# A chunked attention followed by two MLPs on one core: ScalarE's later-block step moved behind unit 1's casts, and six more products of constants on TensorE

## The chip, the cores and the metric

One core of a Trainium2 chip. The metric is the device time of one execution in microseconds (us); the median of several executions is given. TensorE (PE) multiplies matrices, VectorE (DVE), ScalarE (ACT) and GpSimd (POOL) work on tiles, SyncE (SP) issues most of the loads. Each engine takes its instructions strictly in the order in which the program has them and waits for the others by semaphores.

## What is computed

Three stages, one behind the other, all in fp32:

```python
log_a = np.log(np.clip(a, 1e-06, 1.0))            # attention: 4 batches, 8 heads, 768 steps, chunks
for c in range(nc):
    cum = np.cumsum(la, axis=-1)
    L = np.exp(cum[:, :, :, None] - cum[:, :, None, :]) * causal
    M = np.einsum('bhin,bhjn->bhij', Cc, Bc) * L
    y[:, :, sl] = np.einsum('bhij,bhjd->bhid', M, xc) \
        + np.einsum('bhin,bhnd->bhid', Cc, state) * np.exp(cum)[:, :, :, None]
    state = decay_full[:, :, None, None] * state + np.sum(Bx, axis=2)
...
out1 = (silu(x @ w_gate) * (x @ w_val)) @ w_out   # x: 3072 x 256, inner width 1536
...
out[mask] = gate_w[mask, None] * (np.maximum(out1[mask] @ w1[e], 0.0) @ w2[e])   # 8 experts, top 1
```

## The kernel before

The 3072 tokens are cut into 24 **units** of 128 (`NU`) and 6 **blocks** of 512 (`BLK`), four units to a block. A unit goes through: `weigh` (L273, inputs times decay weights: tile xw), `scores_mm` (L286 and L292, 32 small matmuls: the chunk's state sums and C times B), `scores_m` (L300, the causal mask: tile mt), `values_mm` (L338 and L348, 64 small matmuls), `values_out` (L364 to L367, decays put on: tiles y and z; then L369, ScalarE's cast of the unit's output to fp32r: the upper half of xt), `states` (L316, L319 on VectorE, L321, L322 on ScalarE) and `values_low` (L375, the lower half of xt, what the cast left). The MLPs then run each fp32 product as three fp32r products of upper and lower halves.

`first_block` has a **pre-phase** of units 0 to 3, which is all that block 0 needs, and behind it a loop over the MLP's steps of blocks 0 and 1, among which units 4 to 11 are put. In the pre-phase the decays are set up too: `setup_cum(0, 1)` computes for blocks 0 and 1 the exponentials of sums of logarithms (two matmuls passes to a block pair at L192, an exponential on ScalarE at L194: tile er), `setup_cum(1, 2)` those for blocks 2 to 5. `emit_d(b)` spreads er over four rows of constants (tile du; for b = 0 on GpSimd at L254, for b = 1 by four activations on ScalarE at L252), and `emit_u(b, d)` turns that by two matmuls (L265) and two copies on ScalarE (L266) into U, the factor of the unit's outputs. The MLP's weights arrive as 64-bit words, and `decode` makes fp32 of them in four parts: 0 on ScalarE (L400), 1 on VectorE (L403, L404, L406), 2 on ScalarE (L409: wh), 3 on VectorE (L411: wl). `silu_first` (L210) loads ScalarE's table for Silu ahead of its first use. `load(u)` issues two DMAs on SP.

`keep_busy(n)` issues n matmuls of 512 columns on constants (L203), each into the same PSUM tile that nobody reads. They are there for TensorE's clock, which the chip holds at one of two levels, 1.2 and 2.4 GHz; the profile calls the granted level the granted clock (0.50 and 1.00).

The order is written by hand (`manual_schedule`): each engine's queue holds its instructions as the calls below come. Tiles of one `tag` share `bufs` buffers in the order in which they are made, and a new one waits until the readers of the one before it in that buffer are done. Three facts of that kind touch the change: the tag "mt" (two buffers) holds eh, the masked scores of every unit and du; the tag "g" in PSUM (three buffers) holds the results of `setup_cum`, `emit_u` and half of `values_mm`; xt of block 0 is read by the first MLP matmul (L431), which stands behind the last `keep_busy`.

Of the kernel before, what the change touches and what calls it, by code (L numbers as in the profile page):

```python
# [120 lines left out]
def kernel(  # L121
# [17 lines left out]
    def ps_g(name, shape=(128, BLK)):  # L139
        return ps.tile(list(shape), F32, tag="g", bufs=3, name=name)  # L140
# [21 lines left out]
    def load(u):  # L162
        if u >= NU or u in raw:
            return
        r = {}
        xbb = ap_.tile([128, 512], F32, name="xbb", tag="xbb", bufs=4)
        nc.sync.dma_start(out=xbb, in_=I["xbb"][:, u])
        r["x"] = xbb[:, 0:DM].rearrange("k (h d) -> k h d", h=8)
        r["b"] = xbb[:, DM:DM + 128]
        r["bt"] = xbb[:, DM + 128:]  # L170
        r["c"] = ap_.tile([128, 2, 4, 64], F32, name="cbd", tag="cbd", bufs=4)
        nc.sync.dma_start(out=r["c"].rearrange("p r h i -> p (r h i)"), in_=I["cbd"][:, u])
        raw[u] = r

    def setup_loads():
        nc.sync.dma_start(out=at, in_=I["at"])
        nc.scalar.dma_start(out=c1, in_=I["cst"][:, 0:C1])

    def setup_ln():
        nc.vector.tensor_scalar(out=at, in0=at, scalar1=1e-6, scalar2=1.0, op0=ALU.max, op1=ALU.min)  # L180
        nc.scalar.activation(out=at, in_=at, func=AF.Ln)

    def setup_decay():
        p = ps_g("pw", (128, NBLK, 32))
        nc.tensor.matmul(out=p, lhsT=c1[:, C_S:C_S + 128], rhs=at[:, :, 0:32], start=True, stop=True)
        nc.scalar.activation(out=W, in_=p, func=AF.Exp)

    def setup_cum(b0, n):

        p = ps_g("pe", (128, n, 132))  # L190
        for b in range(n):
            nc.tensor.matmul(out=p[:, b], lhsT=at[:, 2 * (b0 + b):2 * (b0 + b) + 2].rearrange("k b c -> k (b c)"),  # L192
                             rhs=c1[:, C_S:C_S + 132], start=True, stop=True)
        nc.scalar.activation(out=er[:, b0:b0 + n], in_=p, func=AF.Exp, scale=-1.0)  # L194
# [3 lines left out]
    def keep_busy(n):  # L198

        if not idle_t:  # L200
            idle_t.append(ps.tile([128, 2, 256], F32, tag="y0", bufs=1, name="pi"))
        for _ in range(n):
            nc.tensor.matmul(out=idle_t[0], lhsT=r32[:, 0],  # L203
                             rhs=r32.rearrange("p g j -> p (g j)").unsqueeze(1).to_broadcast([128, 2, 256]),
                             start=True, stop=True)

    def silu_first():

        t = ap_.tile([128, 1], F32, name="sf")
        nc.scalar.activation(out=t, in_=c1[:, C_ME:C_ME + 1], func=AF.Silu)  # L210

    def setup_ones():
        nc.vector.tensor_copy(out=r16, in_=c1[:, C_R16:C_R16 + 128])
        nc.vector.tensor_copy(out=r32, in_=c1[:, C_R32:C_R32 + 256].rearrange("p (g j) -> p g j", g=2))
# [25 lines left out]
    def cum_store(b0, n, p):  # L240
        nc.vector.tensor_copy(out=eb[:, 8 * b0:8 * b0 + 8 * n], in_=p)
# [5 lines left out]
    def emit_d(b):  # L247
        d = ap_.tile([128, 4, 128], F32R, name="du", tag="mt", bufs=2)
        o = C_MU + 4 * (b % 2)
        if b in (1, 2):  # L250
            for q in range(4):
                nc.scalar.activation(out=d[:, q], in_=er[:, b // 2, 0:128], func=AF.Copy, scale=c1[:, o + q:o + q + 1])  # L252
        else:
            nc.gpsimd.tensor_tensor(  # L254
                out=d, in0=er[:, b // 2, 0:128].unsqueeze(1).to_broadcast([128, 4, 128]),
                in1=c1[:, o:o + 4].unsqueeze(2).to_broadcast([128, 4, 128]), op=ALU.mult)
        return d
# [10 lines left out]
    def weigh(u, e):  # L268

        r = raw[u]  # L270
        b, o = divmod(u, 4)
        r["xw"] = ap_.tile([128, 8, 32], F32, name="xw", tag="xw", bufs=3)
        e.tensor_tensor(out=r["xw"], in0=r["x"], in1=W[:, b, o * 8:o * 8 + 8].unsqueeze(2).to_broadcast([128, 8, 32]),  # L273
                        op=ALU.mult)
# [107 lines left out]
    def load_w(f, e=nc.sync):  # L382
        if f >= NF:
            return
        wr[f] = keep.tile([128, 768, 2], I32, name="wraw", tag="raw", bufs=3)
        e.dma_start(out=wr[f], in_=I["mw"][f].bitcast(I32).rearrange("p (n t) -> p n t", t=2))
# [403 lines left out]
    def first_block():  # L790

        setup_loads()
        load(0)
        load_w(0)
        load(1)
        load(2)
        load_w(1)
        load(3)
        load_w(2)
        nc.sync.dma_start(out=c2, in_=I["cst"][:, C1:C_END])  # L800
        load_w(3)
        setup_ln()
        setup_ones()
        setup_decay()
        setup_cum(0, 1)
        keep_busy(2)
        weigh(0, nc.vector)
        scores_mm(0)
        cum_split(0, 1)
        scores_m(0)  # L810
        emit_u(0, emit_d(0))
        cum_store(0, 1, cum_ends(0, 1, cum_ends_d(0, 1)))
        states(0)
        cum_pairs(1, 8)
        keep_busy(3)
        decode(0, 0)
        for u in range(4):
            weigh(u + 1, nc.vector)
            scores_mm(u + 1)
            values_mm(u)  # L820
            if u == 1:
                setup_cum(1, 2)
            if u == 1:
                d = emit_d(1)
            if u == 2:
                emit_u(1, d)
            keep_busy((5, 7, 6, 10)[u])
            decode(u // 2, 3 if u % 2 else 1)
            scores_m(u + 1)
            if u % 2 == 0:  # L830
                decode(u // 2, 2)
            values_out(u)
            states(u + 1)
            values_low(u)
            if u % 2:
                decode(u // 2 + 1, 0)
            load(u + 4)
            if u == 1:
                silu_first()
        load_w(4)  # L840

        todo = {0: 2, 1: 3, 2: 4, 4: 5, 6: 6, 8: 7, 10: 8, 12: 9, 14: 10, 15: 11}
        units = {0: 4, 1: 5, 3: 6, 5: 7, 13: 8, 16: 9, 19: 10, 22: 11}
        for i in range(2 * NF):
            q, f = divmod(i, HALF)
            b, f = q % 2, f + HALF * (q // 2)
            u = units.get(i)
            w = todo.get(i, NF)
            if i + 1 in units and units[i + 1] > 4:
                weigh(units[i + 1] + 1, nc.vector if i < 16 else nc.gpsimd)  # L850
            if i == 0:
                weigh(5, nc.vector)
            if u == 7:
                scores_mm(u + 1)
                values_mm(u)
                values_out(u)
                values_low(u)
            p = mlp1_mm(b, 0, BLK, f)
            if u is not None and u != 7:
                scores_mm(u + 1)  # L860
                values_mm(u)
            if len(late) == LAG:
                mlp1_down(*late.pop(0))
            late.append((b, 0, BLK, f))
            decode(w, 1)
            h = mlp1_h(p, BLK)
            if w < NF:
                load_w(w + 3)
                decode(w + 1, 0)
            decode(w, 2)  # L870
            if u is not None and u != 7:
                values_out(u)
            decode(w, 3)
            if i >= 20:
                turn_y(0, i - 20)
            mlp1_split(h, b, 0, BLK, f)
            if i in (7, 13):
                take_part(0 if i == 7 else 1)
            if i == 19:
                take_y(0)  # L880
            if u is not None:
                if u != 7:
                    values_low(u)
                    scores_m(u + 1)
                    states(u + 1)
                load(u + 4)
            if i == 6:
                scores_m(8)
                cum_split(1, 2)
            if i == 7:  # L890
                dd.append(cum_ends_d(1, 2))
            if i == 8:
                cum_store(1, 2, cum_ends(1, 2, dd.pop()))
                cum_pairs(8, NU)
                states(8)
            if i == 9:
                dd.append(emit_d(2))
            if i == 10:
                emit_u(2, dd.pop())
            if 16 <= i < 20:  # L900
                setup_route(i - 16)
            if i == 21:
                dd.append(emit_d(3))
            if i == 23:
                emit_u(3, dd.pop())
# [193 lines left out]
```

## Time and profile before

| | us |
|---|---|
| median of 3 executions | 546.77 |
| lowest, highest | 545.44, 546.95 |
| the profiled execution | 547.26 |
| its span, first to last instruction | 545.5 |
| TensorE busy in it | 512.3 (94%) |
| VectorE | 297.8 (55%) |
| ScalarE | 212.7 (39%) |

The profile is of one execution, and its times count from the start of the span. A busy TensorE need not be one at its peak, since matmuls are pipelined. "Issue" in the chain is time in which the engine waited for nothing that the profile shows. The mean granted clock was 0.981.

### The profile page before, as it was taken

How to read it: one execution, taken by the hardware profiler on the slowest of the kernel's cores; microseconds unless marked ns; L12 is line 12 of the kernel's file. 1: busy time of each engine (PE TensorE's matmuls, PEld its weight loads, DVE VectorE, ACT ScalarE, POOL GpSimd, SP SyncE). 2: the span in 40 equal slices, each digit the busy share in tenths (PEclk: the TensorE clock that was granted, in tenths of full speed). 3: DMA queues.
4: the chain of work that ended last, by engine and by line, in shares of the span. 5: the costliest groups of instructions: out<-in, count | busy, mean ns of one | idle time of the engine just before them, and what ended most of it. 6: DMA issues, size and time to landing. Idle time of an engine off the chain costs nothing.

```text
span 545.5 us, 11245 instructions
## 1 busy us (share of the span) xinstructions
PE 512.3 (94%) x4597; PEld 422.2 (77%) x4597; DVE 297.8 (55%) x648; ACT 212.7 (39%) x394; POOL 97.5 (18%) x120
## 2 busy tenths in 40 slices
PE   5699899999999999999999999999997999999990
PEld 3477688778877778887788778888895999899980
DVE  4888787775453554445444554454463755646320
ACT  4644356433232334333433233434442443544320
POOL 0000000121003040004100034211036324250211
PEclk9899899999999999999999999999998999999996
DMA  8755222111030212103100104334056635431100
GB/s 309 263 175 193 100 100 93 40 50 40 22 99 0 62 60 40 40 20 99 21 1 2 41 2 142 92 117 40 20 175 78 186 94 157 146 117 45 38 15 28
DMA packets 20551, 45.85 MB, mean 84 GB/s; under 512 B 4624, under 2 KB 8080, under 8 KB 20496
## 3 DMA queue, kind: packets, MB, share of 16 engines
q1 hardware_dynamic: 17280, 38.39, 23.0%
q0 software_dynamic: 3072, 6.41, 4.5%
q8 instruction: 37, 0.61, 0.6%
q10 hardware_dynamic: 144, 0.30, 0.2%
q14 instruction: 18, 0.15, 0.1%
HBM read 38.59 MB, written 6.50 MB: 83 GB/s over the span
## 4 chain that ended last, share of the span: by engine, by line
PE 76%; issue 11%; DVE 5%; POOL 2%; ACT 2%; DMA 1%; another core or an unknown queue 0%; SPq 0%; POOLq 0%; ACTq 0%
PE py L459 18%; PE pg L431 18%; PE pv L431 17%; PE ph L741 7%; PE po L762 6%; PE pt L543 2%; PE pc L292 2%; POOL out L776 2%; PE py L348 1%; PE py L338 1%; PE pi L203 1%; PE pc L286 1%; PE px L730 1%; DVE hl L446 1%; DMA at<-in_at 1%
## 5 line engine op out<-in xcount | busy, mean ns | idle before, releaser
L431 PE MATMUL pg<-xt,wh 128*128 128x512 f32 x288 | 93.5, 406 | 1.8 <-ACT wh L409 1.8
L431 PE MATMUL pv<-xt,wh 128*128 128x512 f32 x288 | 91.0, 397 | 0.4 <-DVE h L439 0.2
L439 DVE TENSOR_TENSOR h<-h,pv 128x512 f32<-128x512 f32 x72 | 49.4, 686 | 64.1 <-PE pv L431 53.1
L446 DVE TENSOR_TENSOR hl<-h,hh 128x512 fp32r<-128x512 f32 x72 | 50.1, 695 | 62.6 <-ACT hh L445 62.3
L762 PE MATMUL po<-hl,hh 128*128 128x256 f32 x384 | 70.7, 284 | 3.3 <-ACT hh L749 3.3
L741 PE MATMUL ph<-xt,hl 128*128 128x512 f32 x288 | 73.9, 399 | 0.0
L431 PEld LDWEIGHTS pv<-xt,wh 128*128 128x128 f32 x288 | 54.4, 189 | 14.0 <-DVE h L439 0.6
L762 PEld LDWEIGHTS po<-hl,hh 128*128 128x128 f32 x384 | 60.5, 190 | 5.8 <-ACT hh L749 3.8
L431 PEld LDWEIGHTS pg<-xt,wh 128*128 128x128 f32 x288 | 52.4, 190 | 12.4 <-ACT wh L409 2.0
L445 ACT CAST hh<-h 128x512 fp32r<-128x512 f32 x72 | 44.6, 620 | 39.0 <-DVE h L439 39.0
L741 PEld LDWEIGHTS ph<-xt,hl 128*128 128x128 f32 x288 | 52.4, 191 | 9.4
L438 ACT ACTIVATE h<-pg 128x512 f32<-128x512 f32 x72 | 42.7, 593 | 42.0 <-PE pg L431 41.9
L459 PE MATMUL py<-hh,wh 128*128 128x512 f32 x144 | 58.6, 407 | 0.0
L431 PE MATMUL pg<-xt,wl 128*128 128x512 f32 x144 | 57.5, 399 | 0.0
L459 PE MATMUL py<-hl,wh 128*128 128x512 f32 x144 | 56.9, 395 | 0.0
L459 PE MATMUL py<-hh,wl 128*128 128x512 f32 x144 | 56.9, 395 | 0.0
L431 PE MATMUL pv<-xt,wl 128*128 128x512 f32 x144 | 56.8, 394 | 0.0
L601 POOL DMA_INDIRECT slots<-ids,si x24 | 25.4, 1058 | 167.1 <-DVE si L593 162.3
L762 PE MATMUL po<-hl,hl 128*128 128x256 f32 x192 | 54.2, 282 | 0.4 <-DVE hl L750 0.4
L750 DVE SCALAR_TENSOR_TENSOR hl<-ph,hh 128x512 fp32r<-128x512 f32 x48 | 33.1, 689 | 35.5 <-ACT hh L749 33.7
L749 ACT ACTIVATE hh<-ph 128x512 fp32r<-128x512 f32 x48 | 28.8, 600 | 42.3 <-PE ph L741 21.3
L762 PEld LDWEIGHTS po<-hl,hl 128*128 128x128 f32 x192 | 36.2, 189 | 0.9 <-DVE hl L750 0.9
(140 smaller groups left out, 672.0 us busy)
## 6 DMA issues: line engine op xcount, KB each, us to landing
eraw<-in_ew SPq DMA_DIRECT2D x24, 512.0 KB
wraw<-in_mw SPq DMA_DIRECT2D x12, 768.0 KB
xbb<-in_xbb SPq DMA_DIRECT2D x24, 256.0 KB
cbd<-in_cbd SPq DMA_DIRECT2D x24, 256.0 KB
yd<-yr SPq DMA_DIRECT2D x6, 528.0 KB
slots<-ids,si POOLq DMA_INDIRECT x24
xg<-yd,idx POOLq DMA_INDIRECT x24
out<-ob,idx POOLq DMA_INDIRECT x24
```

Of the source, the lines that this page charges most:

```text
L292: nc.tensor.matmul(out=r["pc"][g][32 * q:32 * q + 32, 0:256], lhsT=r["bt"][k, 32 * q:32 * q + 32], rhs=r["c"][k, q // 2].rearrange("p h i ...
L431: nc.tensor.matmul(out=t, lhsT=w[:, f, o:o + 128], rhs=xt[:, xp, k, cs], start=n == 0, stop=n == 5)
L438: nc.scalar.activation(out=h, in_=p[0], func=AF.Silu)
L439: nc.vector.tensor_tensor(out=h, in0=h, in1=p[1], op=ALU.mult)
L445: nc.scalar.copy(out=hh, in_=h)
L446: e.tensor_tensor(out=hl, in0=h, in1=hh.bitcast(F32), op=ALU.subtract)
L459: nc.tensor.matmul(out=yb[b][d][:, c:c + m], lhsT=w[:, f, o:o + 128], rhs=h, start=first and n == 0, stop=last and n == 2, skip_group_chec ...
L601: i = nc.gpsimd.indirect_dma_start(out=slots[0:E * upto], out_offset=bass.IndirectOffsetOnAxis(ap=si[:, s:s + 1], axis=0), in_=ids[g][:, o ...
L741: nc.tensor.matmul(out=p, lhsT=self.hl[:, w, o:o + 128], rhs=self.xt[:, xp, k], start=n == 0, stop=n == 5)
L749: nc.scalar.activation(out=hh, in_=p, func=AF.Relu)
L750: nc.vector.scalar_tensor_tensor(out=hl, in0=p, scalar=0.0, in1=hh.bitcast(F32), op0=ALU.max, op1=ALU.subtract)
L762: nc.tensor.matmul(out=self.po[s // 2][:, s % 2], lhsT=h[:, q], rhs=self.hl[:, w, o:o + DM], start=f == 0 and n == 0 and s % 2 == 0, stop= ...
```

## The change

In the loop over the pre-phase's four units, `setup_cum(1, 2)` and `emit_d(1)` are taken from behind the value matmuls of unit 1 and put, in the other order, at the end of that pass, behind unit 1's output, the states, `values_low`, the first decode step of the next weights and the load of unit 5, and ahead of `silu_first`. On TensorE the two matmuls of `setup_cum(1, 2)` thereby come behind `keep_busy` of unit 1 instead of ahead of it. The counts of `keep_busy` go from 2 to 3, 3 to 4, and in the loop from 5, 7, 6, 10 to 7, 8, 7, 10: six products more in all.

```diff
@@ -803,7 +803,7 @@
         setup_ones()
         setup_decay()
         setup_cum(0, 1)
-        keep_busy(2)
+        keep_busy(3)
         weigh(0, nc.vector)
         scores_mm(0)
         cum_split(0, 1)
@@ -812,19 +812,15 @@
         cum_store(0, 1, cum_ends(0, 1, cum_ends_d(0, 1)))
         states(0)
         cum_pairs(1, 8)
-        keep_busy(3)
+        keep_busy(4)
         decode(0, 0)
         for u in range(4):
             weigh(u + 1, nc.vector)
             scores_mm(u + 1)
             values_mm(u)
-            if u == 1:
-                setup_cum(1, 2)
-            if u == 1:
-                d = emit_d(1)
             if u == 2:
                 emit_u(1, d)
-            keep_busy((5, 7, 6, 10)[u])
+            keep_busy((7, 8, 7, 10)[u])
             decode(u // 2, 3 if u % 2 else 1)
             scores_m(u + 1)
             if u % 2 == 0:
@@ -836,6 +832,8 @@
                 decode(u // 2 + 1, 0)
             load(u + 4)
             if u == 1:
+                d = emit_d(1)
+                setup_cum(1, 2)
                 silu_first()
         load_w(4)
```

## Rows read from the trace of the kernel before

**Rows 1.** The page's head: the span.

```profile
span 545.5 us, 11245 instructions
```

**Rows 2.** The chain that ended last, 4 to 36 us: start, us, what.

```profile
14.05 2.42 issue
...
17.79 0.45 PE py L338 x29
...
18.72 1.04 PE pe L192 x4
...
22.54 0.32 PE pc L286 x10
...
23.29 0.32 PE py L338 x24
...
24.00 0.66 PE pu L265 x2
...
26.04 1.71 issue
...
29.22 2.50 PE pi L203 x10
31.72 1.38 PE pg L431 x6
```

**Rows 3.** Stretches: bounds, us; busy us of each engine (instructions); PEclk, DMA share, GB/s.

```profile
14.10:16.50 2.40, 0.03 (x5) 0.06 (x6) 2.37 (x11) 1.47 (x4) 0.00 (x0) 0.91 1.03 389
16.50:19.50 3.00, 3.00 (x100) 2.49 (x101) 1.91 (x6) 0.00 (x0) 0.00 (x0) 0.50 1.01 393
19.80:26.25 6.45, 5.08 (x111) 3.64 (x109) 4.98 (x14) 6.42 (x14) 0.00 (x0) 1.00 0.48 148
40.00:60.00 20.00, 17.16 (x310) 13.10 (x293) 18.08 (x38) 10.02 (x19) 0.00 (x0) 1.00 0.39 134
60.10:64.80 4.70, 4.66 (x13) 3.24 (x14) 2.76 (x7) 1.47 (x3) 0.00 (x0) 0.64 0.80 279
```

**Rows 4.** TensorE's instructions, 6 to 10 us: start, us, engine, line, operation, tiles.

```profile
6.25 0.78 PE L203 MATMUL pi<-r 128*128 128x512 f32 x1
6.83 0.63 PE L203 MATMUL pi<-r 128*128 128x512 f32 x1
7.39 0.47 PE L286 MATMUL pc<-xw,xbb 64*32 64x64 f32 x16
...
9.80 0.25 PE L236 MATMUL pe<-d,r 128*128 128x32 f32 x1
```

**Rows 5.** VectorE's instructions, 9 to 27 us, with idle time before them.

```profile
9.48 0.18 DVE L229 TENSOR_TENSOR d<-er,c 128x32 fp32r<-128x32 f32 x1
...
16.28 0.95 DVE L411 TENSOR_TENSOR wl<-wv,wh 128x768 fp32r<-128x768 f32 x1
18.32 0.76 DVE L300 TENSOR_TENSOR mt<-pc,c 128x256 f32<-128x256 f32 x2 [1.09 <-PE py L338]
...
19.59 0.28 DVE L367 TENSOR_TENSOR y<-y,z 128x128 f32<-128x128 f32 x1
...
22.02 0.42 DVE L273 TENSOR_TENSOR xw<-xbb,W 128x256 f32<-128x256 f32 x1
...
26.14 0.28 DVE L367 TENSOR_TENSOR y<-y,z 128x128 f32<-128x128 f32 x1
```

**Rows 6.** ScalarE's instructions, 19 to 27 us, with idle time before them.

```profile
19.79 0.39 ACT L194 ACTIVATE er<-pe 128x264 f32<-128x264 f32 x1 [3.73 <-PE pe L192]
...
21.25 0.39 ACT L369 CAST xt<-y 128x256 fp32r<-128x256 f32 x1
...
22.99 1.28 ACT L210 ACT_TABLE_LOAD   x1
...
25.42 0.85 ACT L409 CAST wh<-wv 128x768 fp32r<-128x768 f32 x1
26.45 0.40 ACT L369 CAST xt<-y 128x256 fp32r<-128x256 f32 x1 [0.19 <-DVE y L367]
```

## The prediction

> **What bounds the kernel now.** I read the page's summary first, then the chain that ended last, the stretches with their granted clock, and last the instructions of TensorE, VectorE and ScalarE one by one in the first 32 us, the pre-phase. The span is 545.5 us [rows 1]. In the chain [rows 2] the reader is to see that TensorE is the thread of the pre-phase, but that three times it stands idle and is waited for by nobody ("issue"): 2.42 us before unit 2's scores, again before unit 3's, and 1.71 before unit 4's. What ends each gap is the weighted input of the next unit (xw, L273), the last step of a loop: VectorE's decode, mask and value steps of unit u, then ScalarE's cast of the unit's output (L369), then VectorE's low half (L375), then xw. So an edit gains only what it takes out of that loop. The ten products after unit 3 end at 31.72, where the first MLP matmul starts [rows 2]; from there to 60 us VectorE is busy 18.08 of 20 us [rows 3] with work that started with the pre-phase's end, and no load is late in it. I take it that what the pre-phase gains or loses arrives at the end one to one.
>
> The clock: after the idle time from 14.05 to 16.47 TensorE has 0.50 from 16.5 to 19.5, that is the 1.2 GHz level [rows 3]. Scores and values of unit 2 take 2.25 us there (16.47 to 18.72), those of unit 3 at the 2.4 GHz level 1.46 (22.54 to 24.00) [rows 2].
>
> ScalarE: from 19.80 to 26.25 it is busy 6.42 of 6.45 us [rows 3]. In this stretch stand, in this order, the exponential for the later blocks (L194, 19.79), the four spreads of emit_d(1), unit 1's cast (21.25), two state scalings, a decode step, a table load, two copies of U, wh's cast (25.42), and behind it unit 2's cast (26.45) [rows 6]. That is the fact on which the forecast turns: ScalarE is a second, full thread here.
>
> **The change part by part.**
> *Early products (2 to 3, 3 to 4).* The two products of now start at 6.25 and 6.83, and unit 0's scores right behind them at 7.39 [rows 4]. A third takes another 0.57, the spacing of these three, so the scores start 0.57 later. The spread d (9.48 to 9.66 [rows 5]) moves with them to 10.23; the end sums' matmul, which stands at 9.80 behind POOL's spread and its matmuls, then waits for d and starts at 10.26, 0.46 later [rows 4, 5]. The copy of its result opens a stretch in which VectorE is full until unit 2's xw (2.37 of 2.40 us from 14.10 [rows 3]), so all of unit 0 moves by +0.46. Bounds: 0.34 (the product at some 0.45) to 0.57 (nothing absorbed). The fourth product of the second group runs before xw(1) arrives and costs nothing; without that cover it is 0.23, the price at the upper level (2.50 for ten [rows 2]).
>
> The Trainium skill's TensorE: Matmul & The Clock Gate, section "Wait — 56ns, not 53.3ns?", gives a 512-column matmul at the lower level 426.7 ns from start to start. The row has 0.57, so it doesn't agree here; by the page the delay would be some 0.33 and the forecast 0.13 us lower.
>
> *Two products more after unit 0.* They lie in the 2.42 us gap. TensorE then ends at 14.05 + 0.46 + 2 x 0.23 = 14.97, unit 2's scores start at 16.47 + 0.46 = 16.93, the gap is 1.96. Does the clock still fall? A gap of 2.42 was followed by a fall, one of 1.71 was not [rows 2, 3]; 1.96 lies nearer to the second, and it comes after some 1.9 us of products instead of 1.4. I take: no fall. If it falls, it is a rival below.
>
> *The moved step.* It issues on ScalarE four spreads and one exponential, on TensorE two fp32 matmuls (L192, four passes), nothing on SP or POOL and no DMA; the loads of unit 5 stand on SP where they stood. ScalarE's time isn't made less, only its order. With no fall: unit 2's scores end at 16.93 + 0.75 = 17.68 (22.54 to 23.29 is 0.75 [rows 2]); wl's subtraction ends at 16.28 + 0.95 + 0.46 = 17.69 [rows 5]; the masks start some 0.08 later, 17.77. Now they start at 18.32 and wait for the value products [rows 5]: emit_d's tile sits between the two masks in a tag of two buffers. With emit_d behind the mask that wait is gone, the buffer being that of block 0's spread, long read. Unit 1's last add ends now at 19.87 [rows 5], 1.55 after the masks' start, so then at 19.32, and unit 1's cast starts at 19.36 instead of 21.25 [rows 6]. xw(3), now at 22.02 and 0.77 behind the cast [rows 5, 6], comes at 20.13 and is ready at 20.55.
>
> TensorE sits in front of it, though: the values end at 18.39, eight products make 20.23, and the matmuls of L192 now stand behind the products and ahead of unit 3's scores, some 0.55 at the upper level (1.04 [rows 2] was mostly at the lower one). So unit 3's scores start at 20.8, against 22.54: 1.7 us earlier.
>
> That gain is then mostly lost. ScalarE has the same 6.46 us from its first instruction of the stretch (19.79) to the end of wh's cast (26.25) [rows 6], no shorter in the other order, and starts on it at 19.36. So unit 2's cast starts at 25.82, 0.63 before the 26.45 of now [rows 6]. Its input is long there: unit 2's last add (26.14 + 0.28 [rows 5]) follows xw(3) by 4.4 us: 24.5. The new wait is ScalarE's queue, in front of unit 2's cast, and VectorE idles about 1.2 us for it. What else waits: the second matmul of emit_u(1) needs the PSUM buffer that the exponential reads. What ScalarE does ahead of the table load is the same set as now, so the load (22.99 [rows 6]) starts 0.43 earlier and the exponential, now last before it, ends near 22.6. Seven products and unit 4's scores queue behind that matmul on TensorE; the scores wait for xw(4) until 27.1, so over 2 us cover it. The U copies stand behind the table load as now. One product more in unit 2 lies in the gap as well (0.23 otherwise).
>
> From unit 2's cast on everything keeps its spacing: unit 4's scores 27.75 to 27.12, first MLP matmul 31.72 to 31.09. **Sum: -0.63 us** (the +0.46 is in it; alone it would be a loss). The profiled execution took 547.26 us, so 546.63 by its own time; it lay 0.49 above the median of 546.77, against which I give the forecast: **546.1 us**.
>
> **The rivals.**
> 1. *The clock falls before unit 2 as now.* For it: the gap is still longer than the 1.71 that was survived. Then the scores end at 16.93 + 1.32 = 18.25 (16.47 to 17.79 [rows 2]), masks 18.32, values 19.18, the first value step waits for those, and unit 1's last add ends near 20.13; the cast at 20.17 plus 6.46 is 26.63: +0.18, **547.0 us**. The change then does nothing of what it says.
> 2. *The clock falls before unit 4.* This is the one that ends slower. The seven products after unit 2 end near 24.7 (emit_u's matmuls near 23.1, plus 7 x 0.23), while xw(4) is held up by ScalarE: a gap of 2.4 us, where 1.71 stands now and 2.42 made a fall. Scores and values then take 2.25 instead of 1.46, and the products until the level rises some 0.26 more: +1.05, net +0.42, **547.2 us**. Together with rival 1 it is +1.2, 548.0; if the lower level holds for twice the 3 us of now, into the first MLP group, up to +2.1, 548.9. It becomes slower than now from any extra above 0.63. Against it: unit 3 itself has no gap any more, so TensorE is busy from 20 to 24.7.
> 3. *The fall in block 0 goes too.* From 60.10 to 64.80 the clock is 0.64 and twelve products take 4.7 us [rows 3], where two groups of six at 1.38 [rows 2] make 2.8. If the shift lets that stall pass without a fall: -0.63 - 1.9 = -2.5, **544.2 us**. For it: the runs spread by 1.5 us, about such a price. Against: the stall moves along with all else and isn't made shorter.
>
> **How the numbers follow.** Forecast 0.45, rival 1 0.16, rival 2 0.19, rival 3 0.13, longer falls or several 0.07. A measurement of this kernel tells about 0.3%, 1.6 us, from no change; forecast and rivals 1 and 2 lie within it. So faster 0.14, same 0.79, slower 0.07. The range reaches from rival 3's 544.2 to both falls together with a little less, 547.9; it takes in the early delay's bounds.
>
> **What the changed profile would show.** Right: unit 1's cast at 19.3 to 19.5 and no exponential before it; clock 1.00 from 14 to 32 us; unit 3's scores near 20.8; ScalarE without a gap from there to unit 2's cast near 25.8, with VectorE waiting for that cast; first MLP matmul near 31.1. Wrong: unit 2's cast much before 25.5 (ScalarE's thread then is no bound), 0.50 in a stretch between 26 and 30 us (rival 2) or still from 16.5 (rival 1), unit 0's steps not late by some 0.46, or a first MLP matmul earlier by 1 us with an unchanged end, so that the gain isn't carried through block 0.

## The result: 0.74% slower

The changed kernel took 551.15 us (median of 4; 550.08 to 551.82), the kernel before beside it 546.86 (545.44 to 547.27): a ratio of 1.0074 (95% interval 1.0046 to 1.0102). The forecast was 546.1 with a range to 547.9. In the profiled executions the pre-phase came out nearly as forecast, and 3.7 us were lost 145 us later, at a place that the change does not touch.

The chain that ended last in the changed kernel, 13 to 33 us, as in [rows 2] (start, us, what):

```profile
13.20 1.81 PE pi L203 x7
15.00 1.98 issue
16.98 0.32 PE pc L286 x10
...
18.45 2.04 PE pi L203 x8
20.49 0.45 PE pe L192 x4
20.94 0.27 PE pc L286 x16
...
24.75 2.23 issue
26.98 0.21 PE pc L286
...
28.76 2.51 PE pi L203 x10
31.27 1.40 PE pg L431 x6
```

Unit 2's scores come at 16.98, unit 3's at 20.94 (22.54 before), the first MLP matmul (L431) at 31.27 against 31.72 [rows 2]: 0.45 us earlier. What becomes of that is seen on one instruction of VectorE that both kernels have at the same steps of the MLP (L439), first before, then after (start, us, engine, line, operation, what ended the idle time ahead of it):

```profile
34.61 0.69 DVE L439 TENSOR_TENSOR h<-h,pv 128x512 f32<-128x512 f32 x1 [0.34 <-ACT ha L400]
65.04 0.69 DVE L439 TENSOR_TENSOR h<-h,pv 128x512 f32<-128x512 f32 x1 [1.71 <-PE pv L431]
185.56 0.68 DVE L439 TENSOR_TENSOR h<-h,pv 128x512 f32<-128x512 f32 x1
```

```profile
34.17 0.69 DVE L439 TENSOR_TENSOR h<-h,pv 128x512 f32<-128x512 f32 x1 [0.37 <-ACT ha L400]
64.91 0.69 DVE L439 TENSOR_TENSOR h<-h,pv 128x512 f32<-128x512 f32 x1 [2.01 <-PE pv L431]
189.08 0.69 DVE L439 TENSOR_TENSOR h<-h,pv 128x512 f32<-128x512 f32 x1 [1.24 <-PE pv L431]
```

The shift of after against before is -0.44 us, then -0.13, then +3.52. TensorE's last value matmul of unit 13, during the MLP's block 2, still ends within 0.03 us of the same time in both (174.70 before, 174.67 after). So the loss lies between 175 and 189 us, where the two traces read as follows, before first (VectorE's first two products on those values, then the transposes that follow on TensorE, then stretches with their granted clock as in [rows 3]):

```profile
176.22 0.36 DVE L364 TENSOR_TENSOR y<-py,U 128x192 f32<-128x192 f32 x1 [2.43 <-PE py L348]
178.90 0.29 DVE L365 TENSOR_TENSOR z<-py,U 128x128 f32<-128x128 f32 x1 [2.32 <-PE pg L431]
...
176.63 0.73 PE L543 MATMUL pt<-iw,yT 128*128 128x136 f32 x4 [0.33 <-issue]
...
176.30:179.20 2.90, 2.57 (x14) 2.22 (x14) 0.58 (x3) 0.00 (x0) 0.00 (x0) 1.00 0.02 6
179.20:183.60 4.40, 4.22 (x22) 3.17 (x20) 2.51 (x9) 2.34 (x7) 0.00 (x0) 1.00 0.37 60
```

```profile
178.85 0.36 DVE L364 TENSOR_TENSOR y<-py,U 128x192 f32<-128x192 f32 x1 [5.10 <-remote]
179.12 0.28 DVE L365 TENSOR_TENSOR z<-py,U 128x128 f32<-128x128 f32 x1
...
179.26 0.73 PE L543 MATMUL pt<-iw,yT 128*128 128x136 f32 x4 [3.02 <-DVE y L364]
...
173.74 5.12 another core or an unknown queue
...
176.30:179.20 2.90, 0.00 (x0) 0.00 (x0) 0.35 (x2) 0.00 (x0) 0.00 (x0) 1.00 0.03 6
179.20:183.60 4.40, 4.34 (x14) 3.56 (x15) 2.69 (x10) 2.13 (x6) 0.00 (x0) 0.62 0.35 59
```

VectorE is idle and the values that it needs end at 174.7, but y starts 1.52 us later before and 4.18 us later after. What it waits for is TensorE's signal (a semaphore) that the values are done. The signal is late in both: before, y's gets out after 1.5 us and z's after 4.2; after, both after 4.2. The stretch in which a signal of TensorE that is due does not get out is called the silence below. The transposes need the PSUM buffer that y reads, so before TensorE goes on at 176.63 and hides the rest of the silence under the first layer; after, it has nothing for 3.02 us (the row with 0.00 in 176.30 to 179.20; the chain names the wait "another core or an unknown queue"), and then it works at a clock of 0.62 (14 matmuls in the time of 22). That is 2.7 us more of gap and 1.5 us of clock (the first layer's twelve products in 4.44 us, 179.74 to 184.18, instead of 2.89), of which the next layer gives 0.5 back (there before waits for ScalarE, and after does not). The trace holds one more thing in the silence: one of the loads of 16 KB on queue 8, from 177.57 to 178.52 before and from 177.38 to 178.83 after. The profile calls this an instruction queue (37 loads in all, before as after); that they are TensorE's instructions is taken here, the profile does not name the engine.

### The profile page after: what moved, and what is told of

Read it like the earlier page. It is cut to its first block, busy times and chain, and to the rows that moved or that the text cites. A ratio compares the mean times of both kernels' runs of the same rounds, so it can differ in the third digit from the quotient of the medians.

```text
span 549.9 us, 11259 instructions
## 1 busy us (share of the span) xinstructions
PE 515.1 (94%) x4603; PEld 424.8 (77%) x4603; DVE 297.5 (54%) x648; ACT 212.5 (39%) x394; POOL 97.2 (18%) x120
## 4 chain that ended last, share of the span: by engine, by line
PE 77%; issue 10%; DVE 4%; POOL 2%; another core or an unknown queue 1%; ACT 1%; DMA 1%; SPq 0%; POOLq 0%; DVEq 0%; ACTq 0%
PE py L459 18%; PE pg L431 18%; PE pv L431 18%; PE ph L741 7%; PE po L762 6%; PE pt L543 2%; PE pi L203 2%; PE pc L292 2%; POOL out L776 2%; PE py L348 1%; PE py L338 1%; PE pc L286 1%; PE px L730 1%; DMA at<-in_at 1%
## 5 line engine op out<-in xcount | busy, mean ns | idle before, releaser
L431 PE MATMUL pg<-xt,wh 128*128 128x512 f32 x288 | 93.8, 407 | 1.8 <-ACT wh L409 1.8
L431 PE MATMUL pv<-xt,wh 128*128 128x512 f32 x288 | 91.7, 400 | 0.2 <-DVE h L439 0.2
L439 DVE TENSOR_TENSOR h<-h,pv 128x512 f32<-128x512 f32 x72 | 49.4, 686 | 66.6 <-PE pv L431 54.6
L762 PE MATMUL po<-hl,hh 128*128 128x256 f32 x384 | 71.3, 285 | 3.3 <-ACT hh L749 3.3
L431 PEld LDWEIGHTS pv<-xt,wh 128*128 128x128 f32 x288 | 55.2, 192 | 13.7 <-DVE h L439 0.6
L762 PEld LDWEIGHTS po<-hl,hh 128*128 128x128 f32 x384 | 60.8, 190 | 5.8 <-ACT hh L749 3.8
L431 PEld LDWEIGHTS pg<-xt,wh 128*128 128x128 f32 x288 | 52.7, 190 | 12.5 <-ACT wh L409 2.0
L438 ACT ACTIVATE h<-pg 128x512 f32<-128x512 f32 x72 | 42.8, 594 | 42.7 <-PE pg L431 41.7
L431 PE MATMUL pg<-xt,wl 128*128 128x512 f32 x144 | 57.9, 402 | 0.3 <-DVE wl L411 0.3
L431 PE MATMUL pv<-xt,wl 128*128 128x512 f32 x144 | 57.2, 398 | 0.0
L762 PE MATMUL po<-hl,hl 128*128 128x256 f32 x192 | 54.5, 284 | 0.5 <-DVE hl L750 0.5
L749 ACT ACTIVATE hh<-ph 128x512 fp32r<-128x512 f32 x48 | 28.7, 600 | 42.8 <-PE ph L741 22.2
L762 PEld LDWEIGHTS po<-hl,hl 128*128 128x128 f32 x192 | 36.4, 190 | 0.9 <-DVE hl L750 0.9
```

Of the source, the lines that this page charges most:

```text
L431: nc.tensor.matmul(out=t, lhsT=w[:, f, o:o + 128], rhs=xt[:, xp, k, cs], start=n == 0, stop=n == 5)
L438: nc.scalar.activation(out=h, in_=p[0], func=AF.Silu)
L439: nc.vector.tensor_tensor(out=h, in0=h, in1=p[1], op=ALU.mult)
L749: nc.scalar.activation(out=hh, in_=p, func=AF.Relu)
L762: nc.tensor.matmul(out=self.po[s // 2][:, s % 2], lhsT=h[:, q], rhs=self.hl[:, w, o:o + DM], start=f == 0 and n == 0 and s % 2 == 0, stop= ...
```

## The experiments

The change puts 13 instructions more into TensorE's stream ahead of that place: six products of two each, and one wait (in `emit_u`, L265). The rest of the loss, the last 0.9 us of the span's 4.4, was not followed: the same work, from 418 to 528 us, differs as much between two executions of the kernel before (109.76 and 108.92 us).

The theories: **A**, the place: what decides is at which instruction of TensorE's stream the silence falls; added instructions move it. **B**, the moment: it is the time of the values' end that matters, which the pre-phase's end shifts. **C**, chance: the silence is always there and the first trace of before was lucky. **D**, mass: the more instructions ahead, the later the signals.

The measured values of all. "Count" is the number of TensorE's instructions ahead of unit 13's values, against the kernel before; "y" is y's start less the end of unit 13's values, "gap" the idle time of TensorE ahead of the transposes:

| kernel | count | y, us | gap, us | clock falls near 179 us | time / before (95%) |
|---|---|---|---|---|---|
| before; e5 | 0 | 1.52; 1.48 | 0.33; 0.29 | no; no | |
| after; e12 | +13 | 4.18; 4.57 | 3.02; 3.38 | yes; yes | 1.0074; 1.0067 (1.0053 to 1.0082) |
| e1 | +1 | 4.14 | 2.96 | yes | 1.0046 (0.9998 to 1.0095) |
| e2 | +12 | 4.92 | 3.73 | yes | 1.0104 (1.0023 to 1.0184) |
| e3 | +12 | 4.67 | 3.48 | yes | 1.0115 (1.0052 to 1.0178) |
| e4 | +1 | 3.82 | 2.63 | yes | 1.0038 (1.0002 to 1.0073) |
| e6 | -2 | 1.21 | 0 | no | one execution |
| e7 | -66 | 0.02 | 0 | no | one execution |
| e8 | +93 | 0.02 | 0 | no | one execution |
| e9 | -3 | 1.66 | 0.47 | no | 0.9998 (0.9986 to 1.0010) |
| e10 | +21 | 4.70 | 0 | no | 1.0017 (1.0006 to 1.0028) |
| e11 | +9 | 4.47 | 0 | no | 0.9989 (0.9970 to 1.0007) |
| e13 | -3 | 1.39 | 0.19 | no | 0.9981 (0.9959 to 1.0003) |
| e14 | -1 | 1.38 | 0.20 | no | one execution |
| e15 | +1 | 3.84 | 2.67 | yes | one execution |
| e16; e18 | +2 | 1.35; 1.68 | 0.17; 0.50 | no; no | 1.0024 (0.9994 to 1.0053) |
| e17 | +80 | 0.02 | 0 | no | 1.0036 (1.0002 to 1.0069) |

### The parts of the change alone

e1 makes the move without the added products, e2 adds the products without the move:

```diff
 # e1, against before
-            if u == 1:
-                setup_cum(1, 2)
-            if u == 1:
-                d = emit_d(1)
...
             if u == 1:
+                d = emit_d(1)
+                setup_cum(1, 2)
                 silu_first()
```

> The step moved, the counts of products as before (2, 3 and 5, 7, 6, 10). What is to be told apart is the stall of TensorE in block 2, 3.0 us at 176.2 in the changed kernel and 0.33 us at 176.3 in the one before, in front of the same matmul (L543). Theory A, place: what holds TensorE there hangs on the count of its instructions ahead of that place (the changed kernel has 13 more; the trace shows a load of 16 KB of instructions in the stall). Here it has 1 more: stall below 0.7 us, 546.0 to 547.3 us. Theory B, moment: it hangs on when block 2 comes there (0.43 us earlier in the changed kernel). Then it depends on the pre-phase's end alone: with an end as in the changed kernel the stall is 3 us and the time 550 to 551.5.

```diff
 # e2, against before
-        keep_busy(2)
+        keep_busy(3)
...
-        keep_busy(3)
+        keep_busy(4)
...
-            keep_busy((5, 7, 6, 10)[u])
+            keep_busy((7, 8, 7, 10)[u])
```

> The six products added, the step left where it was. Theory A (place, 12 more TensorE instructions ahead of block 2): a stall of 2.5 to 3.5 us in front of L543 at 176 to 177, a fall of the clock behind it, 549.5 to 552 us. Theory B (moment): the pre-phase ends 0.1 to 0.6 us later than before, no long stall, 546.5 to 547.6.

Each has the gap (2.96 and 3.73 us) and the fall behind it, though each alone makes the pre-phase shorter (the first layer's first matmul starts at 30.60 in e1 and 30.75 in e2, against 31.55 before). e3 leaves the pre-phase as it is and adds the same 12 instructions as products that cost next to nothing; e4 shortens the pre-phase further:

```diff
 # e3, against before
             keep_busy((5, 7, 6, 10)[u])
+            if u == 2:
+                keep_tiny(6)   # matmul of 32 by 64: lhsT=r32[:, 0, 0:32], rhs=r32[:, 0, 0:64]
```

> The kernel before with six small matmuls of 64 columns and 32 weight columns on the same constants behind unit 2's products, where TensorE is idle for 1.7 us: 12 more TensorE instructions and no other change, the pre-phase's end where it was within 0.1 us. Theory A (place): a stall of 2.5 to 3.5 us in front of the first L543 matmul of block 2, 549.5 to 551.5 us. Theory B (moment): as the kernel before, stall 0.3, 546.3 to 547.3 us.

```diff
 # e4, against after
-            keep_busy((7, 8, 7, 10)[u])
+            keep_busy((7, 8, 7, 4)[u])
```

> The changed kernel with 4 instead of 10 products behind unit 3, so that it has as many in all as the kernel before (33) and 1 TensorE instruction more. Theory A (place): stall in block 2 below 0.7 us; pre-phase's end 0.4 to 1.1 us earlier than before, 545.3 to 546.6 us. Theory B (moment): block 2 comes still earlier to its place, stall of 2 us or more, 548.5 to 551 us.

In e3 the values end at 174.76, as before, and the gap is there: B falls. (The 0.43 us in e1's expectation is near the shift at the pre-phase's end; at the values 0.03 was left.) In e1 and e4 one instruction more was enough, where the expectations by A had a gap below 0.7 us. The ratios of e2 and e3 are above the change's, and not all of that is this place: in their traces TensorE's gap near 415 us, of which the last section tells, is 5.6 and 7.7 us, against 3.3 in before and after.

### Place or chance

> The kernel before, unchanged, for a second profiled execution. Theory A (place to the instruction: the added instructions moved the place at which TensorE's stream is cut, and with it the moment at which TensorE's signals stop getting out in block 2): as in the first trace, the gap on TensorE ahead of the four transposes of block 2 (L543, near 176.5 us) is 0.3 to 0.5 us, y's first product (L364) starts within 2 us of the end of the values, the clock does not fall between 175 and 190 us, and the span is about 540. Theory C (the silence of the signals is always there, and the first trace of before got its one signal out by chance): the gap is 2.5 to 3.7 us here too, with a fall of the clock near 179 us, and the time is 3 to 4 us above the median.

```diff
 # e6, against before
-            keep_busy((5, 7, 6, 10)[u])
+            keep_busy((5, 7, 6, 9)[u])
```

> The kernel before with one product of constants fewer at the end of the pre-phase (10 to 9), so TensorE's stream is two instructions shorter from there on. Theory A: the cut moves by two instructions the other way, y's signal gets out as in before, gap ahead of the transposes of block 2 at most 0.5 us, no fall there. Theory C: gap 2.5 to 3.7 us as in the kernels of the first comparison, whatever the count.

```diff
 # e7, against before: the three calls of keep_busy taken out
 # e8, against after
-            keep_busy((7, 8, 7, 10)[u])
+            keep_busy((7, 8, 7, 50)[u])
```

> The kernel before without any of the 33 products of constants: 66 instructions fewer on TensorE. The pre-phase loses its clock, so its own end is not compared (some us later). Theory A: the cut lies 66 instructions later in the work, well behind the transposes of block 2, so the gap ahead of them is 0.3 to 0.5 us, and a silence of the signals of 3 to 5 us turns up later (near 180 to 186 us), where the first layer's products may hide it. Theory C: the silence stays where it is, between the last values of unit 13 and the transposes, gap 2.5 to 3.7 us.

> The changed kernel with 50 instead of 10 products of constants at the end of the pre-phase: 80 instructions more on TensorE, about 9 us more in the pre-phase (40 at 0.22 to 0.23 us) where they hold block 0. Theory A: the cut comes 80 instructions earlier in the work than with the change alone, before the values of unit 13, so the gap ahead of the transposes of block 2 is 0.3 to 0.5 us and the time is 9 us less 3 to 4 us above the change's. Theory C: gap of 2.5 to 3.7 us at the same place in the work, time 9 us above the change's.

VectorE's two products and TensorE's transposes in e6, where one product fewer lets both signals out:

```profile
175.06 0.36 DVE L364 TENSOR_TENSOR y<-py,U 128x192 f32<-128x192 f32 x1 [2.17 <-PE py L348]
175.33 0.28 DVE L365 TENSOR_TENSOR z<-py,U 128x128 f32<-128x128 f32 x1
...
175.47 0.73 PE L543 MATMUL pt<-iw,yT 128*128 128x136 f32 x4
```

In e6 the silence is still there, one wait further on: the transposes end at 176.20, and ScalarE's copy of their result (L545) starts at 179.06, beside the first layer that TensorE runs meanwhile. The kernel before, run again (e5), showed 0.29 us, and with the count moved far either way (e7, e8) y starts 0.02 us behind the values: C falls. So does B once more: the values end at 173.83 in e1 and 173.85 in e6, and only e1 has the gap. In e7 the silence turned up later, as A has it, from 180.6 to 183.9 us, where TensorE ran on under it; and at 206 us, in unit 15's values, TensorE itself stopped in a chain of matmuls that wait for nobody (its rows, and all that moved by DMA in 206.5 to 209.7 us):

```profile
206.16 0.46 PE L348 MATMUL py<-cbd,st 64*32 64x64 f32 x21
208.50 0.24 PE L348 MATMUL py<-cbd,st 64*32 64x64 f32 x1 [1.88 <-issue]
209.78 0.43 PE L348 MATMUL py<-cbd,st 64*32 64x64 f32 x6 [1.04 <-issue]
...
DMA packets 1, 0.02 MB, mean 5 GB/s; under 512 B 0, under 2 KB 0, under 8 KB 0
...
q8 instruction: 1, 0.02, 5.8%
```

5.8% of 16 engines in 3.2 us is one load of 3.0 us, and TensorE stands for nearly as long. e8's time, 558.69 in one execution, can't be set against the others: its 50 last products take 11.60 us where the change's 10 take 2.51, and it has a gap of 1.84 us in block 0 of another kind (wh, L409, late).

### The path from the signal to the time

e9 shortens the stream to 3 below before by leaving out products; e10 takes away what makes the transposes wait for the signal, by putting them ahead of the slice's scores and values; e11 does that to e4; e12 is the change again. The move also puts eight instructions more ahead of the values, so that in e10 and e11 the signal could have come out otherwise; it stayed late.

```diff
 # e9, against after
-            keep_busy((7, 8, 7, 10)[u])
+            keep_busy((7, 8, 7, 2)[u])
 # e10, against after (e11: and with 7, 8, 7, 4)
             p = mlp1_mm(b, 0, BLK, f)
+            early = ahead and f == 4
+            if early:
+                turn_y(b - 1, f - 2)
...
-            if 2 <= f < 6:
+            if 2 <= f < 6 and not early:
                 turn_y(b - 1, f - 2)
```

> The changed kernel with 2 instead of 10 products of constants at the end of the pre-phase (31 products in all): TensorE's stream is 3 instructions shorter than that of the kernel before from there on, as against 13 longer with the change and 1 longer with 4 products there. Theory A (the place of the cut, to the instruction): as with the kernel that was 2 shorter, both signals of unit 13's values get out within 1.5 us, the gap ahead of the transposes of block 2 (L543) is at most 0.5 us and the clock does not fall between 175 and 190 us; the first layer starts 1.2 to 1.5 us earlier than in the kernel before; time against the kernel before 0.995 to 0.999. Theory C (the silence is there whatever the count): gap 2.5 to 3.7 us as with 4 products, time 1.000 to 1.005.

> The changed kernel, with the four transposes of the fifth slice (L543) ahead of the scores and values of that slice in blocks 1 to 3, so that they no longer need the PSUM buffer that VectorE's product y (L364) has to read first. The count of instructions ahead of the values changes by 8 there. If the transposes' need for y's buffer is the path by which the late signal becomes time: y may still start 4 us after the values end, but TensorE goes on into the first layer, with no gap over 0.5 us between 172 and 180 us and no fall of the clock there; time 3 to 4.5 us below the change's, 0.998 to 1.001 of the kernel before. If the late signal holds something else just as long: a gap of 2.5 to 3 us ahead of the first layer's product (L431) in the place of the transposes', time as with the change, 1.004 to 1.010.

> Both: 4 products at the end of the pre-phase, and the fifth slice's transposes ahead of its scores and values. With 4 products alone the first layer started 1.4 us earlier than in the kernel before, and 2.6 us of gap and a fall of the clock took it back. By theory A and the path through y's buffer: no gap over 0.5 us near 175 us, no fall there, time 0.995 to 0.999 of the kernel before. By theory C with another path: a gap of 2 to 3 us elsewhere near 176 us, 1.001 to 1.006.

> The changed kernel itself, on the chip and beside the runs of the three others. Theory A: gap of 2.8 to 3.6 us ahead of the transposes of block 2 and a fall of the clock behind it, in the profile here as in the first, time 1.003 to 1.010 of the kernel before. Theory C (chance of the execution): the gap may be absent here, with 0.998 to 1.002.

On the same chip the change (e12) took 545.93 us, 1.0067 of the kernel before, and e10 542.63, 1.0017: with y as late as ever (first row below) the 3 us are gone, so the gap ahead of the transposes, with the fall behind it, is the path. A new wait took part of it back, which the expectation left out: z is late too, ScalarE's next steps (L438) queue behind the cast of that output, and the first layer's second half waits (TensorE's waits in e10, 172 to 184 us):

```profile
178.63 0.36 DVE L364 TENSOR_TENSOR y<-py,U 128x192 f32<-128x192 f32 x1 [4.47 <-PE pv L431]
...
PE pv L431 <- ACT h L438: 1.6, 1, 1.6
```

e9 escaped the long gap as A said (0.47 us) but gained nothing. In its trace the granted clock in 9 to 60 us is 0.93 (1.00 in the change), and the first layer begins at 30.25 at the lower level, with 0.63 us for a product that takes 0.40 elsewhere. The fall begins in unit 4's work (0.68 from 27.0 to 28.7 us), ahead of the two products at 28.80, behind an idle stretch of 2.23 us that the change has too and passes without a fall; so it is not shown to come from the products left out. That half of its expectation was wrong.

### The count alone

```diff
 # e13, against after
-        keep_busy(3)
+        keep_busy(2)
...
-        keep_busy(4)
+        keep_busy(3)
...
-            keep_busy((7, 8, 7, 10)[u])
+            keep_busy((7, 8, 7, 4)[u])
 # e14, e15: e13 with, behind that line, one or two of e3's small products
+            if u == 3:
+                keep_tiny(1)
 # e16, e18: the kernel before with the same, one; e17: with keep_tiny(40)
```

> The move as in the change, with 31 products of constants (2 and 3 ahead of unit 0, then 7, 8, 7, 4): TensorE's stream is 3 instructions shorter than that of the kernel before. Theory A (the place, to the instruction): both signals of unit 13 get out, gap ahead of the transposes of block 2 (L543) 0 to 0.6 us, at most 0.8 us ahead of the first layer behind it, no fall of the clock between 175 and 190 us; the first layer of block 0 starts 1.2 to 1.9 us earlier than in the kernel before and most of that is kept at the end: time 0.996 to 0.999 of the kernel before. Theory B (not the count but what these kernels do to the times ahead of it): a gap of 2.5 to 3.5 us as with 4 products at the end and 33 in all, time 1.001 to 1.005.

> As e13 with one product of 32 by 64 at the end of the pre-phase (0.03 us): 1 instruction shorter than the kernel before. Theory A: the edge lies between 0 (where y's signal alone gets out, after 1.5 us) and 1 longer, so there is no gap over 0.6 us here. Theory B: the same as e13, whatever that shows.

> As e13 with two products of 32 by 64 at the end of the pre-phase (0.06 us in all): 1 instruction longer than the kernel before, as the two kernels that had a gap. Theory A: y's signal stays in, gap of 2.5 to 3.5 us ahead of the transposes of block 2 and a fall of the clock behind it, 3 to 4 us of span at that place against e13. Theory B: the same as e13, no gap.

> The kernel before with one product of 32 by 64 at the end of the pre-phase: 0.03 us of work, 2 instructions. Theory A: gap of 2.5 to 3.7 us ahead of the transposes of block 2, a fall of the clock behind it, time 1.004 to 1.009 of the kernel before, for 0.03 us of work. Theory B: no gap over 0.5 us, time 0.999 to 1.001.

> The kernel before with 40 products of 32 by 64 at the end of the pre-phase: 80 instructions on TensorE, some 1.2 us of work (0.03 us each) that holds block 0. Theory A (the place): as with 40 large products on the changed kernel, the cut has moved away from unit 13, its signals get out at once, gap ahead of the transposes of block 2 at most 0.5 us and no fall of the clock near 179 us; time 1.000 to 1.003 of the kernel before. Theory D (the more instructions ahead, the later the signals): gap of 3 us or more as with 6 small products, time 1.008 to 1.013.

> The kernel of e16 once more. If the outcome belongs to the kernel: gap of 0.1 to 0.5 us ahead of the transposes, y started 1.2 to 1.6 us after the end of the values. If it is chance so near the edge: a gap of 2.5 to 3.7 us.

e14 and e15 differ by one product of 0.03 us. y and the transposes, e14 first; for e15 also the stretch behind with its clock:

```profile
174.75 0.36 DVE L368 TENSOR_TENSOR y<-py,U 128x192 f32<-128x192 f32 x1 [2.32 <-PE py L352]
...
175.16 0.73 PE L547 MATMUL pt<-iw,yT 128*128 128x136 f32 x4 [0.20 <-issue]
```

```profile
177.26 0.36 DVE L368 TENSOR_TENSOR y<-py,U 128x192 f32<-128x192 f32 x1 [4.74 <-remote]
...
177.67 0.73 PE L547 MATMUL pt<-iw,yT 128*128 128x136 f32 x4 [2.67 <-issue]
...
178.90:182.40 3.50, 3.50 (x10) 2.70 (x9) 2.17 (x6) 1.75 (x5) 0.00 (x0) 0.51 0.39 64
```

One small product, two instructions, goes with 2.5 us more of gap, a fall of the clock, and 3.5 us of time (546.65 and 550.12, one execution each): within this family the count decides. e16 missed its expectation. Two instructions on the kernel before left y's signal out, in e18 again, so the edge lies between +2 and +12 there and between -1 and +1 in the moved kernels. Within each family more instructions never let a signal out sooner until the shift is far: -2 both signals, 0 and +2 one, +12 none; moved, -3 and -1 at least one, +1 to +21 none. That a single number serves for both families was too sharp, and why it differs is open. e16's ratio has 1 inside its interval.

e17 decides between A and D: 80 instructions more on the kernel before, and the silence is gone from the place.

```profile
174.64 0.36 DVE L368 TENSOR_TENSOR y<-py,U 128x192 f32<-128x192 f32 x1 [1.46 <-PE py L352]
174.91 0.28 DVE L369 TENSOR_TENSOR z<-py,U 128x128 f32<-128x128 f32 x1
...
176.06 0.63 PE L547 MATMUL pt<-iw,yT 128*128 128x136 f32 x4
...
176.00:180.00 4.00, 4.00 (x20) 3.31 (x20) 2.17 (x6) 1.58 (x5) 0.00 (x0) 1.00 0.38 47
```

D falls. The time, 1.0036, is a little above the 1.000 to 1.003 that A had for it. An instruction load was under way here too (175.37 to 176.94), and a signal got out in it: the transposes', at 176.70, with ScalarE's copy at 176.72. So a load beside a late signal is what all the late cases have, but not enough by itself. In the nine traces with y late, that load begins 2.3 to 3.0 us after the values have ended, when the signal is overdue already, and y starts between 0.1 us before and 1.1 us after the load's end. What holds the signals in is **not settled**.

No kernel is measurably faster than the one before: e13 and e11 come nearest. e13's first layer starts at 29.43, 2.1 us ahead of before (31.55 in the same view); by the transposes 1.2 us of it are left (175.27 less its gap, 175.08, against 176.30), and at the end 0.19%, with 1 inside the interval.

## Why the prediction was wrong, step by step

*Early products*: unit 0's end sums at 10.32, forecast 10.26. Right. The comparison with the lower level beside it is not borne out: from 6 to 7.5 us both traces have a granted clock of 1.00, though a product takes 0.63 us there, as at 0.50 elsewhere, and the rows do not settle which level it was.

*Two products after unit 0*: an idle stretch of 1.98 us (1.96) and no fall. Right in this trace; the whole pre-phase holds the upper level, which before did not:

```profile
9.00:60.00 51.00, 42.79 (x860) 32.61 (x853) 44.88 (x110) 26.48 (x53) 0.00 (x0) 1.00 0.60 207
60.10:64.80 4.70, 4.44 (x13) 3.28 (x12) 2.33 (x7) 1.04 (x3) 0.00 (x0) 0.64 0.71 265
```

So rivals 1 and 2 did not happen here; the second although TensorE idled 2.23 us before unit 4, near the 2.42 that was followed by a fall before [rows 2, 3]. The reason given, the length of the idle stretch, does not carry this, and the outcome was in part luck. e8, which has the change's instructions up to there, has the same 1.98 us ahead of unit 2 and a clock of 0.54 from 16.8 to 18.0, as rival 1 has it; e9's fall in unit 4's work is rival 2; and e1, with 2.43 us ahead of unit 2 and 2.47 ahead of unit 4, and e17, with 2.43 ahead of unit 2, show no fall. Rival 3 did not happen either: 60.10 to 64.80 has its 0.64 as in [rows 3].

*The moved step*: ScalarE's instructions in after (as [rows 6]):

```profile
19.42 0.41 ACT L369 CAST xt<-y 128x256 fp32r<-128x256 f32 x1 [2.84 <-DVE y L367]
...
22.21 0.36 ACT L194 ACTIVATE er<-pe 128x264 f32<-128x264 f32 x1
22.59 1.28 ACT L210 ACT_TABLE_LOAD   x1
...
25.68 0.41 ACT L369 CAST xt<-y 128x256 fp32r<-128x256 f32 x1
```

Unit 1's cast at 19.42 (forecast 19.36), unit 3's scores at 20.94 (20.8), ScalarE without a gap to unit 2's cast at 25.68 (25.82), VectorE waiting 0.99 us for it (1.2). The bound was the one named. The first MLP matmul came at 31.27 instead of 31.09: unit 4's scores start 0.14 ahead of the forecast, but with its values they take 1.78 us (26.98 to 28.76) where 1.47 was taken over from [rows 2]. **The term -0.63 was -0.45** in this trace; in e12, the same kernel again, the first MLP matmul comes at 31.00 in the chain, and at 31.56 in e5, the kernel before again, so 0.2 us is within what executions differ by.

*"What the pre-phase gains or loses arrives at the end one to one"*: **this step failed**, and with it the forecast. It was taken from block 0 alone [rows 3]. Block 0 already took 0.3 of the 0.45 (VectorE's wait at 65 us is 2.01 instead of 1.71), and at unit 13's values 0.03 was left, so that nearly all of the gain was gone before that signal. Then TensorE's late signal, already in the trace of before, where it cost 0.33 us of gap, cost 3.02 us and a fall of the clock, with 13 instructions more ahead of it: at the next step of the MLP the change was 3.52 us behind. The added instructions were priced by their time only. Rival 2 asked for a loss from another clock fall, but in the pre-phase; no rival had a loss behind block 0. The text's own sign of error, a gain that isn't carried through block 0, did show in part, but the loss that decided lay two blocks on. Why the signal is late at all stays open; that the count moves it, and that the transposes' wait turns it into time, is what the runs show.

## What to carry to other kernels

When a kernel has idle stretches that end with no engine's work ("remote", "unknown queue", "issue") while the inputs have long been there, look at them before any edit that changes the count of instructions ahead of them, however cheap: here one 0.03 us product decided over 3.5 us. Compare a version shifted by a few and by some 80 instructions before the verdict on an edit is believed, and take the next step off the late signal (another order, as in e10) rather than tune the count. And one trace in which the clock did not fall is not yet a property of the kernel: e8 and e9 fell where others with the same idle stretch did not.

## What the hardware showed that I had not expected

TensorE's signals can stay in for 4 us after its matmuls have ended and while it goes on working: in before z's came 4.2 us after the values, with 14 matmuls in 176.30 to 179.20 meanwhile. TensorE itself can stand beside a load of instructions (e7, 1.88 and 1.04 us beside one load of 3.0 us); that the load is the reason is not shown. The Trainium skill's Runtime: NRT & Kernel Launch, section "Instruction fetch mechanics", has instructions refilled in blocks of 16 KiB and calls the cost of crossing into the next mostly hidden. The trace agrees on the size (37 loads, 0.61 MB). On the cost, TensorE is busy 94% of the span of before with 37 such loads in it, but the 2.9 us in e7's unit 15 do not agree.

Executions of one kernel differ at one wait late in the span: TensorE's gap ahead of the second MLP's L762 near 415 us is 3.3 us in before and 2.0 in e5; the changed kernel has 3.3 in the first trace and none over 0.23 us in e12, on the chip of e9 to e12, where the kernel before had a median of 542.11. A fall of the clock follows the 3.3 us (0.60 from 418 to 422 us in before) and not the 2.0 (1.00). Between the two traces of the changed kernel, 551.73 and 545.92 us, nearly all of the difference arises there, from 416 to 427 us. e6, without the gap in block 2, still took 550.12 us in its one execution, with 5.5 us at L762.
